# Where VectorE computes two small tables in a kernel of attention, experts and a gated layer

## The chip, the core and the metric

The kernel runs as one program on one core of a Trainium2 chip. Five engines of that core work side by side, each with an instruction queue of its own that it takes strictly in order: TensorE (PE, whose weight loads are listed apart as PEld), VectorE (DVE), ScalarE (ACT), GpSimd (POOL) and SyncE (SP), which here issues most of the DMA transfers. The metric is device time in microseconds, less is better, as the median of several runs.

## What is computed

Three layers in float32, one behind the other, on 4 x 576 = 2304 tokens:

```python
scores = scale * np.matmul(q, k.transpose(0, 1, 3, 2))        # 4 batches, 8 heads, 576 x 64
thresh = np.max(scores, axis=-1, keepdims=True) - tau
scores = np.where(scores >= thresh, scores, -1000000000.0)
...                                                            # softmax, times v: x is 2304 x 512
expert_idx = np.argmax(x @ w_gate, axis=1)                     # 8 experts
...
for e in range(E):
    mask = expert_idx == e
    xe = x[mask]
    h = np.maximum(xe @ w1[e], 0.0)                            # 512 -> 1024
    ye = h @ w2[e]                                             # 1024 -> 512
    out[mask] = gate_w[mask, None] * ye
...
return (a * b @ w_out)                                         # a = x @ w_a, b = x @ w_b, 512 -> 1536 -> 512
```

## The kernel before

Every float32 operand of a product is split into a high part in a reduced format and a low rest, and a product is three matmuls (high by high, high by low, low by high). So each matrix is made twice in SBUF: ScalarE or GpSimd writes the high part, VectorE or GpSimd subtracts it to get the low part. That is what most of the elementwise work in the trace is: `w<-raw` (weights), `xt_i<-px_i` (an expert's tokens, transposed), `h_i<-ph_i` (the hidden layer, after the ReLU).

**Stage 1, attention.** Its order is written out by hand. The routing runs with it: while a batch's rows are finished, VectorE finds each token's expert, and GpSimd scatters the token's row into a DRAM table `xs`, sorted by expert (line 42, indirect DMA). The last batch's scatters come at the very end of the stage. To fill that end, the first 256 tokens of the fullest expert are computed early (the lead, names beginning with `l_`): eight tiles f = 0 to 7 of 128 hidden units, each with a first layer `l_ph` (line 570), its ReLU and low part `l_h` (lines 574 and 578), and a second layer into `l_py` (line 592); its result leaves as `l_y` (lines 603 and 605).

**Stage 2, the experts.** `ITEMS` lists eight items in falling size: 416, 368, 336, 304, 288, 256, 256 and 256 token slots, one for each expert in the order of its load. `order` makes the table `o_ti` on VectorE (expert, column, row of each item). For item j, `prepare` loads the rows from `xs` into the one buffer `xr_i` (lines 1422 and 1424) and makes four transposing units (line 1437 on TensorE, 1438 and 1439 for the two parts). Then come eight tiles: `first(f)` (line 1455 into `ph_i`, lines 1458 and 1459 for the two parts of `h_i`) and, two tiles later, `second(f)` (line 1472 into four accumulators `py_i`). At the item's last tile the accumulators leave through lines 1477 and 1478 into `y`, and the next item's `second(0)` needs them back. The next item's rows are asked for at f = 1 and transposed from f = 3 on.

Two small computations on VectorE serve later stages. `chunk_list` (lines 1281 to 1315, 36 instructions, names beginning with `o_`) lists the left-over chunks: tokens beyond an item's slots, worked off in a loop after the eighth item, if there are any. `token_ids` (lines 1326 to 1342, 13 instructions, names beginning with `i_`) finds at which column of `y` each token stands, which the gated layer scatters to DRAM.

**Stage 3, the gated layer.** `front` (line 1621) and `back` (line 1644) on TensorE; its weights come as float64 and are converted by `weight64` (lines 1391 to 1402, names `u`, `a`, `t`, `mag`) on VectorE, ScalarE and GpSimd. The first two conversions are written into the experts' stage.

In stages 2 and 3 a scheduler orders the instructions: it walks through the program with its own estimates of durations and gives each engine a fixed queue, taking earlier-written work first when several things are ready. So where a line stands in the program says how early it may go, not where it goes. `tc.issue_after(x)` keeps what is issued under it behind instruction x.

Of the kernel before, what the change touches and what calls it, by code (L numbers as in the profile page):

```python
# [14 lines left out]
ALU = mybir.AluOpType  # L15
# [19 lines left out]
def fr(ap):  # L35
    return ap.bitcast(F32)
# [1132 lines left out]
class Experts:  # L1169
# [273 lines left out]
    def item(self, xt, wunits, n, cols, tag):  # L1443

        nc = self.nc
        st = {}

        def first(f):
            def run():
                st["w", f] = wunits[f]()  # L1450
                w = st["w", f][0]
                ps = self.psh.tile([P, 512], F32, tag="h", name=f"ph_{tag}{f}")
                steps = [(k, a, b) for k in range(4) for a, b in ((0, 0), (0, 1), (1, 0))]
                for s_, (k, a, b) in enumerate(steps):
                    nc.tensor.matmul(ps[:, 0:n], w[a][:, k, :], xt[b][:, k, 0:n],  # L1455
                                     start=(s_ == 0), stop=(s_ == len(steps) - 1))
                hh, hl = [self.hp.tile([P, self.width], F32R, tag=f"h{r}", name=f"h{r}_{tag}{f}") for r in range(2)]
                nc.scalar.activation(hh[:, 0:n], ps[:, 0:n], AF.Relu)
                nc.vector.scalar_tensor_tensor(hl[:, 0:n], ps[:, 0:n], 0.0, fr(hh)[:, 0:n],  # L1459
                                               op0=ALU.max, op1=ALU.subtract)  # L1460
                st["h", f] = (hh, hl)
            return run

        def second(f):
            def run():
                w = st["w", f][1]
                h = st["h", f]
                if f == 0:
                    st["y"] = [self.psy.tile([P, 512], F32, tag=f"y{d}", name=f"py{d}_{tag}") for d in range(4)]
                for d in range(4):  # L1470
                    for a, b in ((0, 0), (0, 1), (1, 0)):
                        nc.tensor.matmul(st["y"][d][:, 0:n], w[a][:, 0, d * P:d * P + P], h[b][:, 0:n],  # L1472
                                         start=(f == 0 and (a, b) == (0, 0)), stop=(f == 7 and a == 1))
                if f == 7:
                    ca, cv = cols()
                    for d in range(4):
                        nc.scalar.copy(self.y[0][:, d, ds(ca, n)], st["y"][d][:, 0:n])
                        nc.vector.tensor_sub(self.y[1][:, d, ds(cv, n)], st["y"][d][:, 0:n],
                                             fr(self.y[0])[:, d, ds(cv, n)])
            return run  # L1480

        return [first(f) for f in range(8)], [second(f) for f in range(8)]

    def experts(self, idt):
        nc, tc = self.nc, self.tc
        with ExitStack() as ctx:
# [7 lines left out]
            def ereg(i):  # L1494
                if i not in regs:
                    regs[i] = nc.sync.value_load(self.ti[0:1, 0, i:i + 1], min_val=0, max_val=E - 1)
                return regs[i]

            def colregs(i):
                def f():  # L1500
                    t = self.ti[0:1, 1, i:i + 1]
                    return [e.value_load(t, min_val=0, max_val=self.NT) for e in (nc.scalar, nc.vector)]
                return f
# [3 lines left out]
            def prepare(j):  # L1507
                i, n = self.ITEMS[j]
                row = nc.sync.value_load(self.ti[0:1, 3, i:i + 1], min_val=0, max_val=E * self.NT - n)
                xr = self.rows(row, n, f"i{j}", self.r["scatters"])  # L1510
                prep[j] = self.xT_units(xr, n, f"i{j}")
# [8 lines left out]
            for j, (i, n) in enumerate(self.ITEMS):  # L1520
                first, second = self.item(prep[j][0], self.expert_weights(ereg(i)) if j else w0, n, colregs(i), f"i{j}")
                nxt = []
                for f in range(8):
                    first[f]()
                    pend.append(second[f])
                    if len(pend) > self.LAG:
                        pend.pop(0)()
                    if j == len(self.ITEMS) - 1 and f in (5, 6):
                        self.gw0.pop(0)()
                    if j == 1 and f == 0:  # L1530
                        self.chunk_list()
                    if j == len(self.ITEMS) - 1 and f == 7:
                        self.nch = nc.values_load(self.mi[0:1, 0:1], min_val=0, max_val=self.NCH)
                    if f == 1 and j + 1 < len(self.ITEMS):
                        prepare(j + 1)
                        nxt = list(prep[j + 1][1])
                    if f >= 3 and nxt:
                        nxt.pop(0)()
# [54 lines left out]
    def gated(self, idt):  # L1593
        nc = self.nc
# [8 lines left out]
        with ExitStack() as ctx:  # L1603
# [4 lines left out]
            w = self.gw  # L1608
            for u in self.gw0:
                u()  # L1610
            ids = self.token_ids(idt)

            def front(g, c0, n):
                res = []
# [117 lines left out]
```

## Time and profile before

| | |
|---|---|
| three runs | median 1121.13 us, 1117.65 to 1121.66 |
| the profiled execution | 1126.54 us, of which 1124.8 us is the span that its trace shows |
| TensorE, matmul | 1056.7 us busy, 94% of the span |
| VectorE | 801.7 us, 71% |
| GpSimd | 686.5 us, 61% |
| ScalarE | 503.9 us, 45% |
| mean granted TensorE clock | 0.98 of full speed |

Times below are microseconds from the start of the span. The profiled execution is 5.4 us above the median of the runs. In it the lead's last tiles run until about 419, the first item's first matmul starts at 420.68, the eighth item's last matmuls end at about 657.5, and the gated layer runs on TensorE from 664.04 on. In windows, a busy time equal to the window's length means an engine that never stood; the column PEclk is TensorE's granted clock, where 1.00 is 2.4 GHz and 0.50 is 1.2 GHz.

### The profile page before, as it was taken

Reading aid. Unit: us, or ns where it says so; the run is one execution under the profiler, and the core shown is the slowest. Engines: PE = TensorE matmul, PEld = TensorE weight load, DVE = VectorE, ACT = ScalarE, POOL = GpSimd, SP = SyncE. Lnnn points to the kernel's source line nnn. Section 1 sums busy time; section 2 is a strip of 40 time slices with the busy share of each in tenths; the row PEclk is TensorE's granted clock in tenths of the full one; section 3 lists DMA queues with packets and bytes.
Section 4 is the critical chain, followed back from the end, with each engine's and each line's share of the span. In section 5 each row is a group of like instructions: output and inputs, shape, how many; then the busy total and the mean of one; then the engine's idle time right before and its main releaser. Section 6 shows DMA issues by size and latency. Waiting matters only on the chain. (4 is left out here: it accounts for less than half of the span.)

```text
span 1124.8 us, 19277 instructions
## 1 busy us (share of the span) xinstructions
PE 1056.7 (94%) x6492; PEld 947.7 (84%) x6492; DVE 801.7 (71%) x1765; ACT 503.9 (45%) x1047; POOL 686.5 (61%) x720
## 2 busy tenths in 40 slices
PE   3899989989988989999999979999999999999996
PEld 3799889979978979999999968888888888888885
DVE  4888888898888787644445799597496794984212
ACT  3788768867856533333334433442231321322110
POOL 3779798888886646555567846455364563654234
PEclk9899999999989998999999989999999999999999
DMA  4478632233222258545556522121011110110012
GB/s 128 116 208 243 188 97 67 77 96 84 69 75 66 86 160 277 174 147 150 159 162 199 161 65 65 49 74 39 20 57 39 38 56 20 57 39 1 10 66 93
DMA packets 105558, 111.81 MB, mean 99 GB/s; under 512 B 16704, under 2 KB 79168, under 8 KB 105456
## 3 DMA queue, kind: packets, MB, share of 16 engines
q1 hardware_dynamic: 101502, 100.79, 31.0%
q0 software_dynamic: 3552, 9.45, 2.2%
q8 instruction: 53, 0.87, 0.3%
q14 instruction: 49, 0.40, 0.1%
q10 hardware_dynamic: 402, 0.29, 0.1%
HBM read 77.47 MB, written 23.08 MB: 89 GB/s over the span
## 5 line engine op out<-in xcount | busy, mean ns | idle before, releaser
L1621 PE MATMUL pg<-y,w 128*128 128x512 f32 (+1 forms) x1440 | 308.6, 373 | 6.5 <-DVEq L1555 6.5
L1621 PEld LDWEIGHTS pg<-y,w 128*128 128x128 f32 x1440 | 253.0, 189 | 58.4 <-ACTq L1555 6.7
L1631 POOL TENSOR_TENSOR g<-gg,g 128x512 fp32r<-128x512 f32 (+1 forms) x60 | 73.3, 1222 | 138.9 <-ACT g L1630 131.4
L1644 PE MATMUL po<-w,g 128*128 128x512 f32 x648 | 152.7, 391 | 0.0
L1644 PEld LDWEIGHTS po<-w,g 128*128 128x128 f32 x648 | 121.2, 188 | 26.2
L717 POOL TENSOR_TENSOR pt<-st,pt 128x512 fp32r<-128x512 f32 x93 | 119.7, 1289 | 28.7 <-ACT pt L707 17.0
L1455 PE MATMUL ph_i<-xt_i,w 128*128 128x256 f32 (+5 forms) x768 | 124.7, 312 | 2.7 <-ACT w L1367 1.7
L1472 PE MATMUL py_i<-h_i,w 128*128 128x256 f32 (+5 forms) x768 | 119.9, 305 | 3.2 <-DVE h_i L1459 1.9
L1455 PEld LDWEIGHTS ph_i<-xt_i,w 128*128 128x128 f32 x768 | 113.2, 191 | 4.2 <-ACT w L1367 1.9
L1472 PEld LDWEIGHTS py_i<-h_i,w 128*128 128x128 f32 x768 | 111.7, 188 | 4.0 <-DVE h_i L1459 2.3
L1628 DVE TENSOR_TENSOR gg<-ga,pg 128x512 f32<-128x512 f32 (+1 forms) x60 | 37.8, 630 | 103.7 <-PE pg L1621 97.3
L1368 DVE TENSOR_TENSOR w<-raw,w 128x512 fp32r<-128x512 f32 x64 | 63.1, 988 | 60.7 <-ACT w L1367 59.3
L1370 POOL TENSOR_SCALAR w<-raw 128x512 fp32r<-128x512 f32 x64 | 50.9, 797 | 86.5 <-DMA raw<-in_moe_w 57.1
L1630 ACT CAST g<-gg 128x512 fp32r<-128x512 f32 (+1 forms) x60 | 34.6, 576 | 149.2 <-DVE gg L1628 79.6
L1401 POOL TENSOR_TENSOR t<-t,w 128x256 f32<-128x256 f32 x72 | 63.7, 890 | 57.8 <-DVE u L1397 26.5
L824 PE MATMUL pv<-pt,sv 128*128 128x288 f32 x512 | 97.4, 313 | 0.8 <-POOL pt L717 0.6
L1371 POOL TENSOR_TENSOR w<-raw,w 128x512 fp32r<-128x512 f32 x64 | 89.3, 1396 | 4.8
L752 PE MATMUL tp<-idf,P 128*128 128x128 f32 x504 | 82.3, 281 | 4.6 <-ACT pt L707 1.5
L1649 DVE TENSOR_TENSOR acc<-acc,po 128x512 f32<-128x512 f32 x90 | 60.5, 683 | 26.8 <-PE po L1644 26.8
L824 PEld LDWEIGHTS pv<-pt,sv 128*128 128x128 f32 x512 | 74.0, 191 | 2.5 <-POOL pt L717 0.8
L1400 POOL TENSOR_TENSOR mag<-a,u 128x256 f32<-128x256 f32 x72 | 60.6, 842 | 24.2 <-DVE a L1398 24.2
L1391 ACT ACTIVATE mag<-raw 128x256 f32<-128x256 f32 x72 | 31.2, 437 | 95.3 <-DVE w L1402 95.2
(267 smaller groups left out, 2079.4 us busy)
## 6 DMA issues: line engine op xcount, KB each, us to landing
raw<-in_moe_w SPq DMA_DIRECT2D x128, 256.0 KB
xs<-zero SPq DMA_DIRECT2D x16, 768.0 KB
raw<-in_moe_w_a SPq DMA_DIRECT2D x12, 512.0 KB
raw<-in_moe_w_b SPq DMA_DIRECT2D x12, 512.0 KB
raw<-in_moe_w_out SPq DMA_DIRECT2D x12, 512.0 KB
kT<-kT SPq DMA_DIRECT2D x32, 160.0 KB
kT<-kT SPq DMA_DIRECT2D x32, 144.0 KB
raw_k<-in_k SPq DMA_DIRECT2D x16, 256.0 KB
```

The source lines that it names most:

```text
L717: nc.gpsimd.tensor_sub(lo, st, fr(hi))
L752: nc.tensor.transpose(st["ps"][:, 128 * j:128 * j + 128], parts(j), idf)
L824: nc.tensor.matmul(R["v", n][:, 0:HALF], lhs, rhs[r], start=(c == 0 and r == 0), stop=(c == 4 and r == 1))
L1368: nc.vector.tensor_sub(lo_t, raw, fr(hi_t))
L1371: self.last_pool = nc.gpsimd.tensor_sub(lo_t, raw, fr(hi_t)).ins
L1400: g.tensor_sub(mag, a.bitcast(F32), u.bitcast(F32))
L1401: g.tensor_sub(t, t, fr(hi))
L1455: nc.tensor.matmul(ps[:, 0:n], w[a][:, k, :], xt[b][:, k, 0:n], start=(s_ == 0), stop=(s_ == len(steps) - 1))
L1472: nc.tensor.matmul(st["y"][d][:, 0:n], w[a][:, 0, d * P:d * P + P], h[b][:, 0:n], start=(f == 0 and (a, b) == (0, 0)), stop=(f == 7 and a ...
L1621: nc.tensor.matmul(ps[:, 0:n], w[g][j][m][a][:, k, :], self.y[b][:, k, c0:c0 + n], start=(s_ == 0), stop=(s_ == len(steps) - 1))
L1631: last = nc.gpsimd.tensor_sub(gl[:, 0:n], gt[:, 0:n], fr(gh)[:, 0:n])
L1644: nc.tensor.matmul(ps, res[j][a][:, t * P:t * P + P], w[g][j][2][b][:, 0, :], start=(s_ == 0), stop=(s_ == len(steps) - 1))
```

## The change

Three places. `chunk_list` is issued behind the low part of the second item's first tile (`self.low`, line 1459), `token_ids` is taken out of the gated layer and issued behind the low part of the third item's first tile, and the second item's rows are asked for at f = 3 instead of f = 1. What they compute is the same.

```diff
-                nc.vector.scalar_tensor_tensor(hl[:, 0:n], ps[:, 0:n], 0.0, fr(hh)[:, 0:n],
-                                               op0=ALU.max, op1=ALU.subtract)
+                self.low = nc.vector.scalar_tensor_tensor(hl[:, 0:n], ps[:, 0:n], 0.0, fr(hh)[:, 0:n],
+                                                          op0=ALU.max, op1=ALU.subtract).ins
...
                     if j == 1 and f == 0:
-                        self.chunk_list()
+                        with tc.issue_after(self.low):
+                            self.chunk_list()
+                    if j == 2 and f == 0:
+                        with tc.issue_after(self.low):
+                            self.ids = self.token_ids(idt)
...
-                    if f == 1 and j + 1 < len(self.ITEMS):
+                    if f == (1 if j else 3) and j + 1 < len(self.ITEMS):
                         prepare(j + 1)
                         nxt = list(prep[j + 1][1])
...
-            ids = self.token_ids(idt)
+            ids = self.ids
```

VectorE's queue at the lead's tiles f = 5 and 6, before (`l_h` is the lead's hidden layer, `l_w` its weights, `o_mc` and `i_pos` belong to the two moved computations, `o_ti` is the items' table, whose loads into registers are the rows of line 1502):

```order
L1267 CAST o_ti<-o_T 128x32
L1284 TENSOR_REDUCE o_m<-o_G_6476 128x8
L1340 TENSOR_TENSOR i_pos<-i_pos,i_a 128x20
L1286 COPY o_mc<-o_m 128x8
L1288 TENSOR_TENSOR o_mc<-o_mc,o_m 128x1
L578 SCALAR_TENSOR_TENSOR l_h_5782<-l_ph,l_h_5782 128x256
L1288 TENSOR_TENSOR o_mc<-o_mc,o_m 128x1
...
L558 TENSOR_TENSOR l_w_5857<-l_raw_5855,l_w_5857 128x512
L1288 TENSOR_TENSOR o_mc<-o_mc,o_m 128x1
...
L1288 TENSOR_TENSOR o_mc<-o_mc,o_m 128x1 x2
...
L578 SCALAR_TENSOR_TENSOR l_h_5859<-l_ph,l_h_5859 128x256
```

The same place now:

```order
L1267 CAST o_ti<-o_T 128x32
L1502 TENSOR_LOAD o_ti
...
L578 SCALAR_TENSOR_TENSOR l_h_5782<-l_ph,l_h_5782 128x256
...
L558 TENSOR_TENSOR l_w_5857<-l_raw_5855,l_w_5857 128x512
...
L578 SCALAR_TENSOR_TENSOR l_h_5859<-l_ph,l_h_5859 128x256
```

Both moved computations have left this stretch; the table's register loads and the lead's own work are all that stays.

TensorE's queue from the lead's tile f = 6 to the first item, before (`px_i` are the transposes of the first item's rows `xr_i`):

```order
L570 MATMUL l_ph<-l_xT,l_w_5833 128x256 x12
L592 MATMUL l_py<-l_h_5782,l_w_5687 128x256 x12
L570 MATMUL l_ph<-l_xT,l_w_5857 128x256 x12
L592 MATMUL l_py<-l_h_5859,l_w_5852 128x256 x12
L1437 MATMUL px_i_6064<-idf,xr_i_6047 128x128 x3
...
L592 MATMUL l_py<-l_h_5859,l_w_5876 128x256 x11
L1455 MATMUL ph_i_6092<-xt_i_6050,w_1_6052 128x416
...
L1455 MATMUL ph_i_6121<-xt_i_6051,w_3_6109 128x416
L1455 MATMUL ph_i_6092<-xt_i_6050,w_1_6053 128x416
```

And now:

```order
L570 MATMUL l_ph<-l_xT,l_w_5833 128x256 x12
L592 MATMUL l_py<-l_h_5782,l_w_5687 128x256 x12
L1437 MATMUL px_i_6064<-idf,xr_i_6047 128x128 x3
...
L570 MATMUL l_ph<-l_xT,l_w_5857 128x256 x12
L592 MATMUL l_py<-l_h_5859,l_w_5852 128x256 x12
L592 MATMUL l_py<-l_h_5859,l_w_5876 128x256 x12
L1455 MATMUL ph_i_6092<-xt_i_6050,w_1_6052 128x416
...
L1455 MATMUL ph_i_6150<-xt_i_6051,w_5_6138 128x416
L1455 MATMUL ph_i_6092<-xt_i_6050,w_1_6053 128x416
```

All sixteen transposes now stand ahead of the lead's last first-layer tile (`l_w_5857`), and six of the first item's matmuls, of three tiles, stand ahead of the first one that needs a low part (`w_1_6053`), where four of two tiles did.

VectorE's queue between the second item's first two `h_i`, now (before, only the two `w` rows stood between them, and the four rows of line 1478 followed without anything between):

```order
L1459 SCALAR_TENSOR_TENSOR h_i_6461<-ph_i_6447,h_i_6460 128x368
L1281 TENSOR_TENSOR o_ov<-o_T,cap 128x8
...
L1368 TENSOR_TENSOR w_25_6697<-raw_6698,w_25_6696 128x512
L1284 TENSOR_REDUCE o_m<-o_G_6476 128x8
...
L1288 TENSOR_TENSOR o_mc<-o_mc,o_m 128x1 x7
...
L1368 TENSOR_TENSOR w_27_6744<-raw_6745,w_27_6743 128x512
L1295 TENSOR_SCALAR o_S<-o_S 128x16
L1459 SCALAR_TENSOR_TENSOR h_i_6549<-ph_i_6535,h_i_6548 128x368
...
L1478 TENSOR_TENSOR y_5981<-py_i_6167,y_5980 128x416
L1296 TENSOR_TENSOR o_C<-io,o_S 128x128
```

Sixteen instructions of the chunk list now stand between the two, one more between the first and the second accumulator's leaving, and the other nineteen behind them, up to the third item's transposes. `token_ids` stands in the same way between the third item's first two `h_i` (eleven of its thirteen instructions), with the last two among the rows of line 1478 that follow.

## Rows read from the trace of the kernel before

**Rows 1.** Timeline, TensorE: start, length, what [idle before <-releaser].
```profile
405.35 1.70 PE L570 MATMUL l_ph<-l_xT,l_w 128*128 128x256 f32 x12 [1.01 <-DVE l_h L578]
406.89 1.60 PE L592 MATMUL l_py<-l_h,l_w 128*128 128x256 f32 x12
410.25 2.75 PE L570 MATMUL l_ph<-l_xT,l_w 128*128 128x256 f32 x12 [1.77 <-DVE l_h L578]
...
414.72 1.96 PE L1437 MATMUL px_i<-idf,xr_i 128*128 128x128 f32 x12
...
417.44 1.57 PE L592 MATMUL l_py<-l_h,l_w 128*128 128x256 f32 x11
420.68 1.74 PE L1455 MATMUL ph_i<-xt_i,w 128*128 128x416 f32 x4 [1.68 <-ACT w L1367]
423.43 8.18 PE L1455 MATMUL ph_i<-xt_i,w 128*128 128x416 f32 x32 [1.01 <-DVE w L1368]
```

**Rows 2.** Windows: busy (count) per engine, PEclk, DMA share, GB/s.
```profile
409.00:410.00 1.00, 0.00 (x0) 0.00 (x0) 0.45 (x3) 0.00 (x0) 0.00 (x0) 1.00 1.05 408
410.00:411.00 1.00, 0.74 (x4) 0.75 (x5) 0.83 (x5) 0.00 (x0) 0.00 (x0) 0.74 1.09 364
413.00:414.00 1.00, 1.00 (x7) 1.00 (x6) 0.54 (x2) 0.38 (x1) 0.00 (x0) 0.55 1.12 327
420.00:421.00 1.00, 0.32 (x1) 0.32 (x2) 0.85 (x2) 1.00 (x3) 1.00 (x2) 0.86 0.94 351
427.00:428.00 1.00, 1.00 (x5) 0.97 (x5) 0.70 (x6) 0.52 (x1) 0.04 (x1) 0.72 1.06 331
423.40:461.00 37.60, 37.57 (x195) 36.87 (x196) 26.74 (x48) 11.51 (x23) 20.62 (x19) 0.94 0.77 244
```

**Rows 3.** Timeline, VectorE, at the lead's tile f = 6.
```profile
405.22 1.10 DVE L1288 TENSOR_TENSOR o_mc<-o_mc,o_m 128x1 f32<-128x1 f32 x1
...
407.36 1.63 DVE L1288 TENSOR_TENSOR o_mc<-o_mc,o_m 128x1 f32<-128x1 f32 x3
409.51 0.35 DVE L1288 TENSOR_TENSOR o_mc<-o_mc,o_m 128x1 f32<-128x1 f32 x2 [0.53 <-DVE o_mc L1288]
409.79 0.42 DVE L578 SCALAR_TENSOR_TENSOR l_h<-l_ph,l_h 128x256 fp32r<-128x256 f32 x1
```

**Rows 4.** SyncE's waits; SyncE's timeline; GpSimd's last scatter; TensorE's queue event of line 1437.
```profile
SPq L1422 <- DMA xs<-xg,si: 0.8, 1, 0.8
406.70 0.37 SPq L1422 DMA_DIRECT2D xr_i<-xs  x1
403.26 1.02 POOL L42 DMA_INDIRECT xs<-xg,si  x1 [0.30 <-issue]
L1437 PEldq EVENT_SEMAPHORE  x1: 51/51/51, 411.6 to 411.6; - x1
```

**Rows 5.** Groups on VectorE, 396 to 428: busy, mean ns.
```profile
L1288 DVE TENSOR_TENSOR o_mc<-o_mc,o_m 128x1 f32<-128x1 f32 x7 | 3.5, 505 | 0.7 <-DVE o_mc L1288 0.5
```

**Rows 6.** Timeline, VectorE and TensorE, first item to second; a window of all engines.
```profile
463.09 0.53 DVE L1459 SCALAR_TENSOR_TENSOR h_i<-ph_i,h_i 128x368 fp32r<-128x368 f32 x1
...
465.84 0.53 DVE L1459 SCALAR_TENSOR_TENSOR h_i<-ph_i,h_i 128x368 fp32r<-128x368 f32 x1
466.29 2.07 DVE L1478 TENSOR_TENSOR y<-py_i,y 128x416 f32 x4
469.74 0.67 PE L1472 MATMUL py_i<-h_i,w 128*128 128x368 f32 x3
461.00:467.00 6.00, 6.00 (x35) 5.96 (x34) 4.63 (x7) 4.36 (x9) 5.75 (x6) 1.00 0.79 233
```

**Rows 7.** The same from the second item to the third.
```profile
500.82 1.87 DVE L1478 TENSOR_TENSOR y<-py_i,y 128x368 f32 x4
503.07 2.00 PE L1472 MATMUL py_i<-h_i,w 128*128 128x336 f32 x12
```

**Rows 8.** Timeline, TensorE, the start of the gated layer.
```profile
664.04 8.26 PE L1621 MATMUL pg<-y,w 128*128 128x512 f32 x23 [6.54 <-DVEq L1555]
```

## Prediction

> **What bounds the kernel now.** I read the page first, then TensorE's timeline, then for each stretch in which TensorE stands the queue that it waits for. TensorE is busy 94% of the span, and from 423.43 on it hardly stands until the eighth item ends: 37.57 of 37.60 us from 423.40 to 461.00 [rows 2]. So a microsecond won or lost on TensorE before that point, or a stall put into that stretch, reaches the end undiminished. Behind the items nothing changes: TensorE stands 6.54 us before 664.04 until VectorE has passed the chunk loop [rows 8], and the orders of all engines are the same there in both kernels, so that stretch only moves with what is ahead of it. The place to look at is the hand-over from the lead to the first item. There TensorE stands 1.01 us before 405.35, 1.77 before 410.25, 1.68 before 420.68 and 1.01 before 423.43 [rows 1]. And the clock answers: after the engine stood from 408.49 to 410.25 the granted clock is at 1.2 GHz from about 410.5 to 413.5 (0.74 in the first of these windows, 0.55 in the last), and after the stop from 419.01 to 420.68 from about 420.9 to 427.7 (0.86, then 0.72) [rows 1, 2].
>
> Who is waited for? The first two stops end with `l_h` on VectorE. For the stop before 410.25 the queue is seen: `l_h` starts at 409.79 behind six `o_mc`, of which one alone takes 1.10 us and three take 1.63 [rows 3]. These are instructions of the chunk list on one column, which nobody needs before the end of the experts' stage. The change takes them away. But that is half of the hand-over. The first item's rows can be asked for only when the last scatter has landed: SyncE waits 0.8 us for it, the scatter was made at 403.26, the load goes out at 406.70, and TensorE's queue passes the event of line 1437, the first transpose's, at 411.6 [rows 4]. None of these times depends on the moved work.
>
> **The change, part by part, against the profiled execution's 1126.54 us.**
>
> *The lead's end.* Without the moved instructions the stop before 405.35 shrinks; the table `o_ti` comes earlier, but the register loads that now stand directly behind it keep VectorE and ScalarE a little longer ahead of `l_h`, so I leave 0.25 of the 1.01 us. `l_ph` of tile 6 and `l_py` behind it (1.70 and 1.60 us [rows 1], overlapping by 0.15) then end near 407.7 instead of 408.49. Next in TensorE's queue, though, is no longer the lead's tile 7 but the sixteen transposes, and their rows are there at 411.6. So TensorE stands 3.9 us where it stood 1.77, and goes on 1.35 us later than before (411.6 against 410.25). Left to do up to the lead's last matmul are the transposes (1.96 us for twelve, 2.6 for sixteen), one `l_ph` and two `l_py` (1.6 each): 7.4 us at 2.4 GHz, so 419.0 at the best; before it was 417.44 + 1.57 = 419.01. After a stop of 1.77 us the clock was low for 3 us; after a longer one I count at least that, and 1.5 us for 3 us at half speed: 420.5. So the lead ends 0 to 1.5 us later; I take 0.7.
>
> *The first item's start.* From the lead's last matmul to the first of the item goes the same chain as before (`l_y`, then the weights' high part on ScalarE, 1.68 us). Then six matmuls run ahead of the first low part instead of four. At 1.74 us for four [rows 1], the two more cover 0.87 of the 1.01 us stop; on VectorE the list's instruction that stood among these rows is gone as well. I take −0.9, between −0.7 and −1.0. The third tile's weights, which were asked for behind the second item's rows, now go out ahead of them; that wait did not show on TensorE before. The low clock from 420.9 to 427.7 costs half of the 5.8 us in it that TensorE worked, 2.9 us. With no second stop in it I expect it to end some 3 us earlier: −1.5 at the best, 0 at the worst; I take −0.9. Together with the lead's end: +0.7 − 0.9 − 0.9 = −1.1, between −2.5 and +0.8.
>
> *The second item's start.* Here the list is not free. VectorE must read the first item's accumulators (four times 0.52 us from 466.29) before TensorE reuses them at 469.74 [rows 6]: the first is out at 466.8, 2.9 us ahead, and two more `ph_i` matmuls now stand in front, so 3.3. Into VectorE's queue ahead of them come sixteen instructions. Such an instruction took 0.18 us when GpSimd had nothing to do (two in 0.35 [rows 3]), 0.505 in the mean of the seven `o_mc` [rows 5]: 2.9 to 8.1 us. VectorE has about 0.9 us of idle time in front of 466.29 (4.63 of 6.00 us busy from 461 to 467), and GpSimd is busy 5.75 of these 6.00 [rows 6], so the dear end is the nearer one for the list's eleven two-operand instructions and the cheap one for the other five: 5.6 + 0.9 − 0.9 = 5.6, less 3.3, is 2.3. At the cheap price all is hidden. Since the two operands of `o_mc` also wait for each other, which the other instructions do less, I take 1.0 between 0 and 2.3.
>
> The Trainium skill ("SBUF — State Buffer", Who interferes with whom) says that a VectorE instruction with two SBUF inputs and a GpSimd instruction that reads SBUF exclude each other for a whole instruction. The slow `o_mc` [rows 3] agree with it; by that rule alone the sum would be nearer to +2 than to +1 at this place.
>
> *The third item's start.* The same with `token_ids`: eleven instructions, 2.0 to 5.6 us, ahead of accumulators that were out at 500.82 + 0.47 = 501.3 and wanted at 503.07 [rows 7], 1.8 us of cover and 0.3 from two matmuls moved in front. That is 0 to 3.5 us; I take 0.7. Behind both places the queue has room again: `h_i` is wanted two tiles after it is made.
>
> *The moved rows, conversions and register loads.* The second item's rows now go out behind the third tile's weights and the first two float64 weights, and the latter's first conversions stand on VectorE ahead of the first `h_i`. No row shows TensorE waiting for these transfers or conversions before, and the transposes come a tile after the rows are asked for; I count 0, with up to 0.5 us for a late low part.
>
> **Sum:** −1.1 + 1.0 + 0.7 = **+0.6 us**, 1127.1 in that execution's terms. The median of the runs is 5.4 us lower, so **1121.7 us**. Ends: −2.5, and +0.8 + 2.3 + 3.5 + 0.5 = +7.1, in which all goes wrong at once.
>
> **Rivals.**
>
> *The whole hand-over closes (faster).* Were VectorE the only cause, the stops of 1.01, 1.77 and 1.01 us would go, and both stretches of low clock with them (1.5 and 2.9 us): −8.2, 1112.9 us. For it: the trace names VectorE at three of the four stops. Against: the rows at 411.6 are not VectorE's. It needs TensorE to have work until they land.
>
> *The accumulators (slower).* If both computations go at GpSimd's pace, TensorE stands 2.3 us and then 3.5 us, and each such stop lowers the clock as the one of 1.77 us did, for 3 us, 1.5 us each: 2.3 + 3.5 + 3.0 − 1.1 = +7.7, 1128.8 us. The point that decides is the cover of 3.3 and 2.1 us; it turns as soon as a list instruction costs over 0.26 us in the mean (3.3 + 0.9 by sixteen). For it: GpSimd is busy all through both places. Against: the scheduler put matmuls in front where it expected lateness.
>
> *Nothing to be seen.* The scatter, the rows and the `l_y` chain fix the hand-over, and the accumulators' cover holds: 0, 1121.1 us.
>
> **How the numbers follow.** Chances: my sum 0.72, the closed hand-over 0.08, the late accumulators 0.10, nothing 0.10. A change under 0.5%, 5.6 us, can't be told from none in this kernel, and both my sum and the last rival lie in it. So: faster 0.08, same 0.82, slower 0.10. Range: my sum's bounds give 1118.6 to 1128.2; its upper corner is unlikely, the runs of before alone span 4 us, so 1117.0 to 1126.5.
>
> **What would show it.** Right: TensorE standing 3 to 4 us in front of the first transposes with no `o_mc` before them; the clock low after it; no stop of 1 us behind the first matmuls of the item; a stop at the first `py_i` of the second and third items, released by `y` on VectorE. Wrong: transposes that start before 410, or a lead that ends before 418 (then faster); stops over 2 us at the items' starts with a low clock behind (then slower); or a first `py_i` of the first item that waits for `h_i` behind the conversions.

## The result, and the profile after

The changed kernel took 1128.85 us in the median of 11 runs (1123.36 to 1135.57), the kernel before 1121.66 (1117.65 to 1129.03, 11 runs). The ratio is 1.0054, 95% interval 1.0035 to 1.0073: about 6 us slower, where 1121.7 us and no difference that can be told were forecast. The profiled execution of the changed kernel took 1129.57 us, its span is 1127.9 us.

TensorE's timeline of the changed kernel, from the lead's tile f = 6 to the fourth item (start, length, what, and in brackets the idle time before it and its releaser):

```profile
405.56 1.70 PE L570 MATMUL l_ph<-l_xT,l_w 128*128 128x256 f32 x12 [1.58 <-DVE l_h L578]
407.10 1.60 PE L592 MATMUL l_py<-l_h,l_w 128*128 128x256 f32 x12
411.01 2.28 PE L1437 MATMUL px_i<-idf,xr_i 128*128 128x128 f32 x16 [2.31 <-DMA xr_i<-xs]
413.22 2.73 PE L570 MATMUL l_ph<-l_xT,l_w 128*128 128x256 f32 x12
415.79 3.02 PE L592 MATMUL l_py<-l_h,l_w 128*128 128x256 f32 x24
420.49 1.69 PE L1455 MATMUL ph_i<-xt_i,w 128*128 128x416 f32 x6 [1.68 <-ACT w L1367]
422.60 7.38 PE L1455 MATMUL ph_i<-xt_i,w 128*128 128x416 f32 x30 [0.43 <-DVE w L1368]
...
456.16 2.16 PE L1455 MATMUL ph_i<-xt_i,w 128*128 128x368 f32 x12
...
470.48 0.75 PE L1472 MATMUL py_i<-h_i,w 128*128 128x368 f32 x3 [1.90 <-DVE y L1478]
...
492.37 2.01 PE L1455 MATMUL ph_i<-xt_i,w 128*128 128x336 f32 x12
...
506.34 0.70 PE L1472 MATMUL py_i<-h_i,w 128*128 128x336 f32 x3 [2.70 <-DVE i_pos L1340]
```

The upper rows answer to [rows 1]. The stop of 1.77 us at the lead's last `l_ph` is gone, and a wait of 2.31 us for the first item's rows stands ahead of the transposes. The stop of 1.01 us inside the first item has become 0.43. The two last rows have no counterpart before: TensorE stands 1.90 us ahead of the second item's second layer and 2.70 us ahead of the third's, where it went on without a stop before ([rows 6, 7]).

Windows of the changed kernel (busy time and count of each engine, then the granted clock, the DMA share and GB/s), behind the rows' wait, behind the first item's start, and behind the third item's stop:

```profile
412.00:414.00 2.00, 2.00 (x12) 1.61 (x11) 0.41 (x1) 0.95 (x3) 0.00 (x0) 0.54 1.12 331
...
424.00:426.00 2.00, 2.00 (x8) 1.92 (x7) 2.00 (x3) 0.00 (x0) 1.38 (x1) 0.55 0.95 268
426.00:428.00 2.00, 2.00 (x13) 1.98 (x12) 1.86 (x7) 1.15 (x3) 0.00 (x0) 1.00 1.06 391
...
507.00:509.00 2.00, 2.00 (x12) 2.00 (x11) 1.86 (x5) 0.00 (x0) 0.86 (x2) 0.68 0.56 191
509.00:511.00 2.00, 2.00 (x9) 2.00 (x9) 1.09 (x2) 0.97 (x2) 1.03 (x1) 0.50 0.44 131
```

The low stretch in the first item now ends by 426, where it lasted to 427.7 before ([rows 2]). A new one, at 1.2 GHz from about 507.7 to 511, follows the third item's stop.

What the releasers stand for is in VectorE's timeline of the changed kernel, at the second item's start and at the third's:

```profile
461.23 0.53 DVE L1459 SCALAR_TENSOR_TENSOR h_i<-ph_i,h_i 128x368 fp32r<-128x368 f32 x1
...
462.01 1.79 DVE L1368 TENSOR_TENSOR w<-raw,w 128x512 fp32r<-128x512 f32 x1
...
464.35 3.70 DVE L1288 TENSOR_TENSOR o_mc<-o_mc,o_m 128x1 f32<-128x1 f32 x7
...
468.63 0.68 DVE L1368 TENSOR_TENSOR w<-raw,w 128x512 fp32r<-128x512 f32 x1
...
469.30 0.53 DVE L1459 SCALAR_TENSOR_TENSOR h_i<-ph_i,h_i 128x368 fp32r<-128x368 f32 x1
469.75 0.58 DVE L1478 TENSOR_TENSOR y<-py_i,y 128x416 f32 x1
...
498.16 0.49 DVE L1459 SCALAR_TENSOR_TENSOR h_i<-ph_i,h_i 128x336 fp32r<-128x336 f32 x1
...
499.16 1.52 DVE L1368 TENSOR_TENSOR w<-raw,w 128x512 fp32r<-128x512 f32 x1
...
501.81 0.82 DVE L1334 TENSOR_TENSOR i_a<-slot,i_a 128x20 f32<-128x20 f32 x1
...
503.51 1.73 DVE L1368 TENSOR_TENSOR w<-raw,w 128x512 fp32r<-128x512 f32 x1
...
505.25 0.49 DVE L1459 SCALAR_TENSOR_TENSOR h_i<-ph_i,h_i 128x336 fp32r<-128x336 f32 x1
505.67 0.52 DVE L1478 TENSOR_TENSOR y<-py_i,y 128x368 f32 x1
```

In the second item 8.1 us pass from the first `h_i` to the second (461.23 to 469.30), in the third 7.1 (498.16 to 505.25); before it was 2.75 in the second (463.09 to 465.84, [rows 6]). Only then come the `y` that read the old item's accumulators. TensorE needs those accumulators back, and so it stands. Not all of the added time is the tables' own. Before, the same two places on VectorE held nothing but these `w`, in the second item and then in the third:

```profile
463.54 0.68 DVE L1368 TENSOR_TENSOR w<-raw,w 128x512 fp32r<-128x512 f32 x1
464.79 1.13 DVE L1368 TENSOR_TENSOR w<-raw,w 128x512 fp32r<-128x512 f32 x1 [0.57 <-ACT w L1367]
...
498.10 0.68 DVE L1368 TENSOR_TENSOR w<-raw,w 128x512 fp32r<-128x512 f32 x1
499.26 1.22 DVE L1368 TENSOR_TENSOR w<-raw,w 128x512 fp32r<-128x512 f32 x1 [0.48 <-ACT w L1367]
```

The two `w` of the second item take 2.47 us now (1.79 and 0.68) where they took 1.81, those of the third 3.25 (1.52 and 1.73) where they took 1.90.

**Where the time lies.** From the two timelines: the second item's first `ph_i` starts at 456.16 where it was 457.82 (−1.66). The second item, from its first `ph_i` to the third's, takes 36.21 us where it took 34.13 (+2.08). The third takes 36.74 where it took 32.29 (+4.45: 2.70 of stop, the rest low clock). From the fourth item to the gated layer's first matmul, at 668.27, it is −0.64, and the gated layer to the end of the span −1.13. The sum is +3.1, the difference of the two spans. The medians lie 7.2 us apart, about 6 by the ratio, because the execution of before that was profiled was 4.9 us above its median, this one 0.7. A better partner is the trace of `lead_alone` (below), which has the queues of the kernel before and ran at 1122.69 us: its second item starts at 456.17, its items take the same 34.13 and 32.29 us, and its gated layer starts at 661.23. Against it the changed kernel gains nothing in the hand-over, and 6.5 of the 7.0 us to the gated layer lie in the second and the third item.

### The profile page after: what moved, and what is told of

It is laid out like the page before. It is cut to its first block, busy times and chain, and to the rows that moved or that the text cites. A ratio compares the mean times of both kernels' runs of the same rounds, so it can differ in the third digit from the quotient of the medians.

```text
span 1127.9 us, 19281 instructions
## 1 busy us (share of the span) xinstructions
PE 1053.9 (93%) x6492; PEld 944.9 (84%) x6492; DVE 806.7 (72%) x1765; ACT 504.9 (45%) x1047; POOL 686.1 (61%) x720
## 5 line engine op out<-in xcount | busy, mean ns | idle before, releaser
L1626 PEld LDWEIGHTS pg<-y,w 128*128 128x128 f32 x1440 | 252.2, 189 | 58.1 <-ACTq L1560 6.7
L1368 DVE TENSOR_TENSOR w<-raw,w 128x512 fp32r<-128x512 f32 x64 | 66.9, 1048 | 50.5 <-ACT w L1367 50.2
L1367 ACT CAST w<-raw 128x512 fp32r<-128x512 f32 x64 | 39.6, 622 | 83.2 <-DMA raw<-in_moe_w 47.4
```

The costliest lines, as they stand in the source:

```text
L1368: nc.vector.tensor_sub(lo_t, raw, fr(hi_t))
L1626: nc.tensor.matmul(ps[:, 0:n], w[g][j][m][a][:, k, :], self.y[b][:, k, c0:c0 + n], start=(s_ == 0), stop=(s_ == len(steps) - 1))
```

## The experiments

The theory is the prediction's second rival, the accumulators: the price is TensorE's stop while `y` stands behind the tables, with the low clock that may follow. Against it stand contention (the tables' work costs as much wherever it stands in the items) and the hand-over (the loss comes from the rows' load and the transposes). Ratios are to the kernel before, with 95% intervals.

**Both tables behind the last `y`** (`behind_exit`):

```diff
+                        self.exitv = nc.vector.tensor_sub(self.y[1][:, d, ds(cv, n)], ...).ins
...
-                    if j == 1 and f == 0:
-                        with tc.issue_after(self.low):
+                    if j == 1 and f == 1:
+                        with tc.issue_after(self.exitv):
...
-                    if j == 2 and f == 0:
-                        with tc.issue_after(self.low):
+                    if j == 2 and f == 1:
+                        with tc.issue_after(self.exitv):
```

> Both tables stay at the starts of the second and third items, but each is queued behind the last of the four y subtractions with which the item before leaves the accumulators, and no longer behind the first-layer subtraction of the new item's first tile. Everything else is as in the changed kernel. Theory (the accumulators' exit): the two stops of TensorE at py_i, 1.90 us before the second item's and 2.70 us before the third item's second layer, shrink to under 0.7 us, the granted clock stays at 1.00 after the third item's start, and 2.1 + 4.5 = 6.6 us come back: about 1122 us, a ratio to the kernel before of 0.997 to 1.002. Rival (contention: the tables' 10 us on VectorE beside TensorE's work cost what they cost wherever they stand in the items): the ratio stays at 1.004 to 1.007, and the idle time turns up at other instructions. Rival (the hand-over and the rows' load are the loss): the ratio stays at 1.004 to 1.007, and the stops at py_i go without the time going.

Measured: 0.9987 (0.9973 to 1.0001), 1122.39 us. TensorE's timeline of this kernel, second and third item:

```profile
455.47 2.16 PE L1455 MATMUL ph_i<-xt_i,w 128*128 128x368 f32 x12
...
467.39 0.67 PE L1472 MATMUL py_i<-h_i,w 128*128 128x368 f32 x3
...
489.60 2.01 PE L1455 MATMUL ph_i<-xt_i,w 128*128 128x336 f32 x12
...
500.72 2.00 PE L1472 MATMUL py_i<-h_i,w 128*128 128x336 f32 x12
...
521.89 1.84 PE L1455 MATMUL ph_i<-xt_i,w 128*128 128x304 f32 x12
```

No bracket stands behind either `py_i`: there is no stop. The items take 34.13 and 32.29 us, those of the kernel before to the hundredth, with every instruction of the tables still on VectorE at the items' starts. Nor are they cheaper there in the third item, where GpSimd works on beside them: the same eleven instructions of `token_ids` take 5.3 us in all, 4.2 in the changed kernel. Two of them (the first is the one that took 0.82 us above, the other took 0.17 there):

```profile
503.62 1.22 DVE L1334 TENSOR_TENSOR i_a<-slot,i_a 128x20 f32<-128x20 f32 x1
...
505.83 1.13 DVE L1339 TENSOR_TENSOR i_a<-i_a,i_b 128x20 f32<-128x20 f32 x1
```

In the second item the list is cheaper (its seven additions take 1.5 us in sum, 3.5 in the changed kernel; GpSimd stands from 467.2 to 469.7). That is the theory's result, and the third item rules out contention as the loss: dearer instructions, and no stop. The order, one tile later in the queue, brings back 7.5 us by the ratios (1.0054 less 0.9987) and 7.0 by the gated layer's start (668.27 less 661.30), 6.5 of them in the two items.

**One table each way** (`list_at_start`: only the tokens' part of the edit above):

```diff
-                    if j == 2 and f == 0:
-                        with tc.issue_after(self.low):
+                    if j == 2 and f == 1:
+                        with tc.issue_after(self.exitv):
```

> The chunks' list stands where the changed kernel has it, behind the second item's first tile; the tokens' columns are queued behind the last of the y subtractions in the third item. Theory (the accumulators' exit): the second item keeps its stop of about 1.9 us with the clock at 1.00, the third item's goes, so 4.5 of the 6.6 us come back: a ratio to the kernel before of 0.999 to 1.004, some 2.1 us above the kernel in which both tables stand behind the exit. Rivals (contention, hand-over): a ratio of 1.004 to 1.007, no different from the changed kernel.

Measured: 1.0008 (0.9994 to 1.0022), 1124.93 us. The second item takes 35.89 us with a stop of 1.56 released by `y`, the third 32.29. The list's place costs 2.4 us by the ratios and 1.8 in the trace (35.89 less 34.13), the tokens' 5.2 by the ratios and 4.5 in the traces (36.74 less 32.29). The interval still reaches that of `behind_exit`; the list's share rests on the trace.

**The rows' load alone, undone and done.** `rows_as_before`:

```diff
-                    if f == (1 if j else 3) and j + 1 < len(self.ITEMS):
+                    if f == 1 and j + 1 < len(self.ITEMS):
```

> Only the third part of the change is undone: the second item's rows are loaded at tile two again, the tables stay as the changed kernel has them. Theory (the accumulators' exit): both stops at py_i stay (1.9 and 2.7 us, the clock low after the second), and the time stays within 1.5 us of the changed kernel's: a ratio to the kernel before of 1.004 to 1.007. Rival (the hand-over and the rows' load are the loss): the time goes back to that of the kernel before, a ratio of 0.998 to 1.002. Rival (contention): 1.004 to 1.007 as by the theory.

`rows_alone` is the kernel before with the opposite edit of that line:

> Only the third part of the change is done: the second item's rows are loaded at tile four, and both tables stand where the kernel before has them. Theory (the accumulators' exit): neither the hand-over's stop of 1.01 us nor anything at the items' starts changes, and the ratio to the kernel before is 0.998 to 1.002. Rival (the hand-over and the rows' load are the loss): a ratio of 1.003 to 1.007. Rival (contention from the tables): 0.998 to 1.002.

Measured: 1.0058 (1.0045 to 1.0071) and 1.0005 (0.9991 to 1.0019). Neither way does the rows' load move the time by an amount that can be told, so the hand-over theory falls. One thing came out otherwise than I expected. The third item's stop stayed (2.8 us, clock 0.64 from 504 to 508), but the second item's was all but gone (34.22 us), and another had come ahead of it. TensorE and VectorE of `rows_as_before`:

```profile
450.76 2.54 PE L1455 MATMUL ph_i<-xt_i,w 128*128 128x416 f32 x12 [1.36 <-DVE h_i L1459]
...
467.67 0.74 PE L1472 MATMUL py_i<-h_i,w 128*128 128x368 f32 x3
```

```profile
448.34 1.26 DVE L1394 TENSOR_SCALAR u<-a 128x256 int32<-128x256 int32 x1
...
461.51 2.30 DVE L1288 TENSOR_TENSOR o_mc<-o_mc,o_m 128x1 f32<-128x1 f32 x7
```

The float64 conversions now stand ahead of an `h_i` late in the first item (1.36 us of stop), and the seven `o_mc` happened to take 2.30 us instead of 3.70, so that the list was hidden there. So the unchanged time is a sum of two movements: the first item takes 37.12 us where the changed kernel's takes 35.67, the second 34.22 where it takes 36.21.

**A shorter stop** (`tokens_halved`: as `behind_exit`, with `token_ids` split in two):

```diff
         v.tensor_tensor(a, r["slot"], a, op=ALU.subtract)
+        yield
...
+                    if j == 2 and f == 0:
+                        two = self.token_ids(idt)
+                        with tc.issue_after(self.low):
+                            next(two)
                     if j == 2 and f == 1:
                         with tc.issue_after(self.exitv):
-                            self.ids = self.token_ids(idt)
+                            self.ids = next(two)
```

> As the kernel with both tables behind the exit, but the first six of the tokens' eleven instructions (through the first subtraction) stay behind the third item's first tile, ahead of the y subtractions; the other five follow them. It asks what a shorter stop costs. Theory (the 4.5 us of the third item are a stop of 2.7 us and 1.8 us of low clock that follow from a stop that long): the five instructions taken away were some 1.7 us of VectorE's time, so the stop at py_i shrinks from 2.7 to about 1.0 us, the granted clock stays at 1.00, and the time is about 1 us above the kernel with both tables behind the exit: a ratio to the kernel before of 0.998 to 1.001. Rival (any stop at the items' starts brings the clock down): 1.0 + 1.8 us, a ratio of 1.000 to 1.003, with a row of the clock near 0.6 behind the third item's start. Rival (the tables' cost does not go with the stop): as the changed kernel's, 1.003 or more.

Measured: 1.0011 (0.9993 to 1.0028), 1123.59 us; in the trace a stop of 1.25 us at the third item, the clock at 1.00 all along, the item 33.78 us, 1.49 above the undisturbed 32.29. The trace is the theory's; the ratio lies 2.7 us above `behind_exit`, between the theory's 1 and the rival's 2.8, and its interval holds both.

**More and less of the list.** `list_chain_twice` does the running sum twice, `list_sums_short` does it in three instructions on 64 elements:

```diff
         v.tensor_copy(mc, m)
         for i in range(1, E):
             v.tensor_tensor(mc[:, i:i + 1], mc[:, i - 1:i], m[:, i:i + 1], op=ALU.add)
+        v.tensor_copy(mc, m)
+        for i in range(1, E):
+            v.tensor_tensor(mc[:, i:i + 1], mc[:, i - 1:i], m[:, i:i + 1], op=ALU.add)
```

```diff
-        v.tensor_copy(mc, m)
-        for i in range(1, E):
-            v.tensor_tensor(mc[:, i:i + 1], mc[:, i - 1:i], m[:, i:i + 1], op=ALU.add)
+        v.tensor_tensor(G, row(io), col(io), op=ALU.is_le)
+        v.tensor_tensor(G, G, row(m), op=ALU.mult)
+        v.tensor_reduce(mc, G, axis=AX.X, op=ALU.add)
```

> The changed kernel, with the copy and the seven running additions of the chunks' list done a second time (the same result again), 4 us more on VectorE at the second item's start, of which about 2.4 us fall ahead of the last y subtraction. Theory (the accumulators' exit): the second item's stop grows from 1.9 to about 4.3 us and the granted clock now falls behind it too, as it did in the third item after 2.7 us, so the time is 2.4 + 1.8 us above the changed kernel: a ratio to the kernel before of 1.007 to 1.011. Rival (the stops have slack behind them, the loss is elsewhere): the ratio stays at 1.004 to 1.007.

> The changed kernel, with the list's running sum made by three instructions on 64 elements (a comparison, a product and a sum, 0.2 us each by the list's other instructions of that size) in place of the seven dependent additions of one element (3.70 us); same result. The list's later instructions move up into part of the room, so that some 2.0 us less stand ahead of the y subtractions. Theory (the accumulators' exit): the second item's stop shrinks from 1.9 us to under 0.5, the third item's stays (2.7 us), and the time is 1.5 to 2.2 us below the changed kernel's: a ratio to the kernel before of 1.003 to 1.005. Rival (the second item's stop is covered by slack further on): no gain, 1.005 to 1.007.

Measured: 1.0064 (1.0041 to 1.0088) and 1.0049 (1.0025 to 1.0073). Both miss, for two reasons. The first is that neither edit changed by much what stands ahead of the `y`, because the scheduler filled the queue anew. With the doubled sum, only a copy and two of the second seven additions stand there, and five instructions of the list that stood there have gone behind; with the short one, three later ones have moved up, and a fourth of 1.30 us stands between the first and the second `y`. From the new item's first `h_i` to the first `y` pass 8.5 us in the changed kernel, 8.3 and 8.2 in these two, and the second item takes 36.21, 35.94 and 36.27 us. That fits the theory and does not test it: neither the time ahead of `y` nor the item's length moved. The second is that an instruction of the list has no fixed price. Durations in ns (least, median, greatest) of the seven additions in the changed kernel:

```profile
L1288 DVE TENSOR_TENSOR o_mc<-o_mc,o_m x7: 159/162/1155, 464.3 to 467.9; 128x1 f32<-128x1 f32 x7
```

and of the second seven in the doubled list, with GpSimd's timeline of that kernel at this place:

```profile
L1291 DVE TENSOR_TENSOR o_mc<-o_mc,o_m x7: 146/152/161, 463.7 to 467.5; 128x1 f32<-128x1 f32 x7
```

```profile
461.79 1.29 POOL L1374 TENSOR_TENSOR w<-raw,w 128x512 fp32r<-128x512 f32 x1
468.05 1.13 POOL L1373 TENSOR_SCALAR w<-raw 128x512 fp32r<-128x512 f32 x1 [4.96 <-PE py_i L1475]
```

While GpSimd stands from 463.1 to 468.0 the same addition takes 0.15 us, so the doubled seven were nearly free. Where it works, what counts is whether one of its instructions is running when the addition starts. One of the seven in the changed kernel, and GpSimd beside it:

```profile
464.54 1.15 DVE L1288 TENSOR_TENSOR o_mc<-o_mc,o_m 128x1 f32<-128x1 f32 x1
```

```profile
464.37 1.31 POOL L1371 TENSOR_TENSOR w<-raw,w 128x512 fp32r<-128x512 f32 x1
```

It starts inside the GpSimd instruction and ends with it, within 0.02 us (465.69 and 465.68). This holds without an exception in the thirteen traces that have these additions, those of before and of `lead_alone` among them: 25 of the 98 started while a GpSimd instruction ran, took 0.45 to 1.24 us and ended within 0.02 us of its end; the other 73 took 0.15 to 0.16. And in the short version the product on 64 elements took 1.35 us and one instruction on 16 elements 0.90, where I had counted 0.2.

**Does the stop lower the clock?** Two further executions of the changed kernel:

> The changed kernel once more, for the granted clock behind the third item's stop alone. If a stop of 2.7 us brings the clock down every time, the windows from 505 to 513 us show a mean below 0.8 again. If it does so only in some executions (the kernel with the longer list had a stop of 2.56 us there and a clock of 1.00 behind it), one of the two looks can show 1.00 throughout, and the third item's start then takes 1.8 us less.

> As the other look at the changed kernel: a clock below 0.8 behind the third item's stop in both if the stop alone decides, 1.00 in one or both if it does not.

Windows behind the third item's stop, in the first of them (stop 2.65 us, ending at 506.34), then in the second (stop 3.05 us, ending at 502.26):

```profile
507.00:509.00 2.00, 2.00 (x15) 2.00 (x14) 1.86 (x5) 0.36 (x1) 1.22 (x2) 1.00 0.60 198
509.00:511.00 2.00, 2.00 (x15) 1.77 (x14) 1.36 (x2) 0.61 (x3) 1.21 (x2) 1.00 0.49 136
```

```profile
504.00:506.00 2.00, 2.00 (x9) 2.00 (x8) 0.93 (x3) 0.80 (x2) 1.28 (x1) 0.50 0.24 73
506.00:508.00 2.00, 2.00 (x12) 1.99 (x11) 0.97 (x2) 0.18 (x1) 0.03 (x2) 0.75 0.56 175
```

Only in some executions. Of six traces with this stop, of four kernels, three have the low clock behind it (third item 36.74 to 37.12 us) and three do not (35.04 to 35.13). So the stop costs 2.8 us over the undisturbed 32.29, and the clock, when it falls, about 1.8 more. Those with the fall are those with the longer stops (2.70 to 3.05 against 2.56 to 2.65), and at this place alone length could be what decides. At two others it is not. At the transposes of the changed kernel the clock fell after waits of 2.31 and 2.62 us and stayed at 1.00 after 2.54 (second further execution). At the lead's last `l_ph` it fell after 1.77 us before [rows 1, 2] and stayed at 1.00 after the same 1.77 us in `lead_alone`. What does decide stays open.

**The hand-over's remaining wait.** In `lead_first`, which is `behind_exit` with one edit more, the first item's transposes are queued behind the lead's last `l_ph` tile:

```diff
-                    nc.tensor.matmul(ps, w[a][:, k, :], st["xT"][b][:, k, :], ...)
+                    self.routing["lead_mm"] = nc.tensor.matmul(ps, w[a][:, k, :], st["xT"][b][:, k, :], ...).ins
...
-            for f in prep[0][1]:
-                f()
+            with tc.issue_after(self.r["lead_mm"]):
+                for f in prep[0][1]:
+                    f()
```

> Both tables behind the exit, and the first item's sixteen transposes are queued on TensorE behind the lead's last l_ph tile, no longer ahead of it, so that the 1.6 to 1.9 us of that tile and some of the l_py behind it lie in the wait for the rows' load (0.8 to 2.5 us in the kernels run so far). Theory of the hand-over: the wait at px_i for the load goes or falls under 0.5 us, the lead ends 1 to 2.5 us earlier, and the first item's stop for its weights stays at about 1.7 us: 0.5 to 2.5 us below the kernel with both tables behind the exit, a ratio to the kernel before of 0.996 to 0.999. Rival (the first item is paced by its weights' arrival, not by the lead's end): the stop ahead of ph_i grows by what the lead gains, and the ratio stays at 0.998 to 1.000.

`lead_first_rows` adds the one-line edit of `rows_as_before` to it, and `lead_alone` puts only the edit just shown into the kernel before:

> As the kernel with the lead's tile ahead of the transposes and both tables behind the exit, but with the second item's rows loaded at tile two, as in the kernel before. Theory: the rows' place is worth nothing either way, so within 1.5 us of that kernel: a ratio to the kernel before of 0.996 to 1.000. Rival (the earlier load takes the slots of the first item's weights on the DMA queue and delays them): 1 to 2 us above it.

> The kernel before, with one thing changed: the first item's sixteen transposes are queued on TensorE behind the lead's last l_ph tile. The tables stand where the kernel before has them, through the lead's end. It asks how much of the gain of the kernel with both needs the tables moved away. Theory: the transposes' wait for the rows' load is filled, worth 1.5 to 2.5 us, but VectorE's subtraction of the lead's last tile stands behind the running additions again (it stopped TensorE for 1.0 us at the tile before), so a part comes back: a ratio to the kernel before of 0.997 to 1.000. Rival (the whole of the gain is the lead's order, the tables are worth nothing): 0.9965 to 0.998, as with both. Rival (the gain needs the tables moved): 0.999 to 1.001.

Measured: 0.9973 (0.9954 to 0.9992) for `lead_first`, 1119.29 us; 0.9983 (0.9967 to 0.9999) with the rows as before, 1120.73; 1.0004 (0.9983 to 1.0026) for `lead_alone`, 1124.38. The first two are the only kernels here whose intervals end below the kernel before. TensorE's timeline of `lead_first`:

```profile
405.26 1.70 PE L570 MATMUL l_ph<-l_xT,l_w 128*128 128x256 f32 x12 [1.09 <-DVE l_h L578]
...
408.24 1.60 PE L570 MATMUL l_ph<-l_xT,l_w 128*128 128x256 f32 x12
...
411.12 1.97 PE L1437 MATMUL px_i<-idf,xr_i 128*128 128x128 f32 x12
...
417.09 8.63 PE L1455 MATMUL ph_i<-xt_i,w 128*128 128x416 f32 x36 [1.68 <-ACT w L1367]
```

The transposes start at 411.12 without a wait, where the changed kernel's start at 411.01 after one: the rows arrive when they do, and the lead's tiles now fill the time. From the first of these rows to the first item pass 11.8 us. In the two further executions of the changed kernel it is 15.2 and 13.7, the first with the low clock behind the transposes' wait and the second without.

In `lead_alone` the additions are back in front of `l_h`:

```profile
410.04 1.70 PE L570 MATMUL l_ph<-l_xT,l_w 128*128 128x256 f32 x12 [1.77 <-DVE l_h L578]
...
413.02 1.97 PE L1437 MATMUL px_i<-idf,xr_i 128*128 128x128 f32 x12
...
421.74 8.25 PE L1455 MATMUL ph_i<-xt_i,w 128*128 128x416 f32 x32 [1.11 <-DVE w L1368]
```

The old stops of 1.77 and 1.1 us stand there again. But this run doesn't test what it was meant to. In the kernel before, the transposes already stand behind the lead's last `l_ph` ([rows 1]: 414.72 behind 410.25, without a wait), and only the change put them ahead of it. The edit changes nothing there: the traces of `lead_alone` and of the kernel before have the same instructions in the same order on TensorE, VectorE, ScalarE and GpSimd. Its 1.0004 is the kernel before measured once more, and the order's worth without the tables' move stays untested.

What can be said comes from the kernels in which the tables are moved. `lead_first_rows` is in effect the kernel before with both tables behind the exit, since TensorE's order is the same in both through the hand-over: 0.9983, with the moved rows besides (`lead_first`) 0.9973. So moving the tables was worth 2 to 3 us where the transposes kept their place. `behind_exit`, with the transposes ahead of the tile, is at 0.9987. That this place cost some 1.6 us there is shown by the wait in the traces (0.78 to 3.44 us in the kernels that have it, none with the tile ahead) and not by the ratios, whose intervals overlap.

## Why the prediction was wrong, point by point

*What bounds the kernel, and the hand-over.* The place and the order of events were right; the sum came near by luck. The lead ends at 418.81, in a trace that stands 0.24 us earlier than that of before already ahead of the hand-over; forecast was 0 to 1.5 later than 419.01. The stop before 405.35 did not shrink to 0.25 but stayed at 1.58 (1.1 in both further executions), and the transposes waited 2.31 us (2.5 to 2.6), not 3.9, since the rows were there at 411.0. Inside the first item the stop shrank by 0.6 (forecast 0.9) and the low clock ended about two microseconds earlier. In all −1.66, or −1.4 beside the 0.24; forecast −1.1. Much of that is the clock of one execution: from the lead's tile that starts near 398 to the second item pass 59.6 us in the trace that the prediction read, 58.2 in `lead_alone` with the same queues, and 58.2, 58.1 and 55.0 in the three executions of the changed kernel.

*The second item's start.* The mechanism was the one forecast, VectorE's `y` behind the list; the term was mis-sized: +1.0 taken, +2.08 measured (1.90 of it the stop), inside its bounds of 0 to 2.3. It was not the list that came out dearer than taken. Between the two `h_i` its sixteen instructions took 5.15 us, the seven additions 3.70 (0.53 each, the dear end) and the nine others 1.45 (0.16 each, the cheap one); by the prediction's own sum, less 0.9 of idle time and 3.3 of cover, that is 0.95, the 1.0 that it took. The step that failed is that the list was counted alone. The two `w` among it took 0.66 us longer than before, for which the sum has no term, and of the 0.9 us of idle time only 0.57 lay between the two `h_i`.

The prediction set the Trainium skill's rule on two SBUF inputs ("SBUF — State Buffer", Who interferes with whom) beside the sum, for the list, and did not follow it; by it the sum would have been nearer to +2, and +2.08 came, though not by the list. `w` has two such inputs too, and the rows agree: the one of 1.79 us starts at 462.01 inside a GpSimd instruction that ends at 463.26, and ends 0.54 us behind it.

*The third item's start.* This is the term that failed most: +0.7 taken, bounds 0 to 3.5, measured +4.45 in the profiled execution, 2.70 of stop and 1.75 of low clock. The 0.7 implies 0.25 us for each of the eleven instructions (0.7 and 2.1 of cover); between the two `h_i` they took 3.43 us, 0.31 each. The cover was 1.8 us, not 2.1, because 22 first-layer matmuls stand ahead of the first `py_i` in both kernels (499.69 before, 500.11 now), so that nothing was moved in front here. The two `w` took 1.35 us longer, which had no term. 3.43 and 1.35, less 0.48 of idle time and 1.8 of cover, is 2.5 of the 2.70. And the clock, which the prediction priced at 1.5 us a stop for its rival, was not in the bounds of its own sum at all: it cost 1.75 us in that execution, nothing in others. Taking 0.7 from 0 to 3.5 had no row behind it, and no row on GpSimd at this place was read; in the trace of before it works from 494.87 to 504.6 with no break over 0.1 us.

*The moved rows.* 0 forecast, and by two experiments no difference that can be told. In one of them two movements cancelled, a stop of 1.36 us behind the conversions and a second item 1.99 us shorter.

*The rivals.* "The accumulators" got 0.10 and 1128.8 us; the median is 1128.85. It is right in place and mechanism, and the number is luck: the stops are 1.9 and 2.7 us, not 2.3 and 3.5, and the clock falls behind one of them, and not every time. Its point of decision, 0.26 us for an instruction of the list in the mean, was passed: the sixteen took 5.15 us (461.68 to 469.30, less 1.79 and 0.68 of two `w`), 0.32 each; alone they would have cost the 0.95 us above. "The whole hand-over closes" failed for the reason given against it, the rows at 411.

*The chances.* Given what was read (GpSimd busy in 5.75 of 6 us, a dear end of 0.505 us measured), the cheap end needed a reason and the dear one did not, and a low clock behind a stop had been seen twice in the rows; the rival should have had most of the chance.

## What to carry to other kernels

Small work is moved off a stop by looking at what will stand behind it in the same queue: here the reads that give back the accumulators had about 3 and 2 us of cover, and behind them the same work cost nothing. When a cheap and a dear price for an instruction have both been measured, take the one whose neighbours (here GpSimd's work beside it) are those of the new place, and price anew what already stands there: 0.66 of the one stop's 1.90 us and 1.35 of the other's 2.70 went with `w` that grew longer. Before an edit is taken for a test, compare the queues that it makes: `lead_alone` made those of the kernel before, and the two edits of the list hardly changed the time ahead of `y`.

## What the runs showed of the hardware

A VectorE addition on one column took 0.15 to 0.16 us when no GpSimd instruction was running at its start (73 of 98, in thirteen traces), and otherwise lasted until that GpSimd instruction ended, within 0.02 us (the other 25, 0.45 to 1.24 us). Instructions with one tensor operand were caught too (0.90 us on 16 elements at line 1295 of `list_sums_short`, 0.17 elsewhere). The Trainium skill ("SBUF — State Buffer", Who interferes with whom) says of `tensor_scalar` that it can do so in a two-port mode, and of `tensor_reduce` that it never does; the sums over 160 elements (line 1327) do stay at 0.30 to 0.32 us throughout. And stops of TensorE at the same instruction were followed by 1.2 GHz in some executions and by 2.4 GHz in others, after 1.77 us either way at the lead's last `l_ph` with the same queues; behind the third item's stop it is worth some 1.8 us.
